# The state product k^T v of a gated linear attention, written as two 48-column matmuls in two halves of TensorE's array instead of one of 112 columns

## The chip, the cores and the metric

The kernel runs on one core of a Trainium2 chip, in one launch. The metric is the device time in microseconds, the median of several runs. A core has five engines with an instruction queue each: PE (TensorE, matrix products into PSUM), DVE (VectorE), ACT (ScalarE), POOL (GpSimd) and SP (SyncE, which here issues the DMAs). In the profile a matmul leaves two kinds of records: PEld, the load of the stationary operand into the array, and PE, the streaming of the moving operand.

## What is computed

A gated linear attention over 4 batches of 8 heads, 768 steps and 48 channels, and behind it a feed-forward layer (384 to 2048 to 384) on its 3072 tokens. Per head:

```
S_re, S_im = (ar * S_re - ai * S_im) + k[t] v[t]^T,  ar * S_im + ai * S_re
y[t] = q[t]^T S_re                    # 48 x 48 state, one step after the other
h = x @ w_in;  g = h * sigmoid(1.702 * h);  out = g @ w_out
```

## The kernel before

The complex decay is taken out of the recurrence: q and k are rotated by the running phase and scaled by the running magnitude beforehand (`prepare`). A head then has 48 cosine rows and 48 sine rows. They are put, by DMA, into rows 0 to 47 and 64 to 111 of a 112-row operand `qkh`, and rows 48 to 63 hold zeros.

The tokens are worked in 12 units of 256 (three units to a batch), each unit in two chunks of 128. For a chunk, `attend` puts these steps on PE, each in two groups of four heads (`hh`):

- scores (L690, out `p_ps`): eight matmuls a group, each 64 stationary columns, which write to partitions 0 to 63 or 64 to 127 in turn; four of them stream 128 columns and four stream 64. DVE masks the result into `pm` (L694).
- mix (L716, out `x_ps`): matmuls of 32 stationary columns, four of them in the four quarters of the array, over `pm` and the state `st`.
- turn (L736, out `k_ps`): four transposes of k, 112 rows, which ACT copies to `kt` (L745).
- zed (L742, out `z_ps`): the state product, four matmuls a group, the lines that the change touches. Each takes `kt` of a head, 112 columns wide, as the stationary operand, and streams the head's 48 columns of v, so that it writes 112 partitions by 48 columns. DVE then adds `z_ps` to the state (L750, L754). No step follows the last chunk of a batch, so there are 20 chunks with this product: 40 groups and 160 matmuls.

The feed-forward layer of a unit (`moe`) consists of L780 (`h_ps`, 128 stationary columns, 256 moving) and L810 (`o_ps`, 128 stationary, 384 moving). In unit 0 its operands are plain float32 (`x`, `valA`, `valU`, `g`); from unit 1 on both operands are split in two parts of a shorter format and three products are summed (`xhi`, `xlo`, `hiA`, `loA` and so on).

A record of PE is not a matmul: a plain float32 matmul, as in L690, L716 and L742, leaves two PE records and two PEld records, one pair for each of two passes. So a group of four in L742 has 8 records.

The order of all instructions is planned beforehand (`Plan`), by durations that stand in the code: `add("PE", 0.44, ...)` for a group of L742. The change leaves these numbers alone, and the instructions of every engine stand in the same order after it. So what stands beside a group of L742 is the same as before. Counted over the 40 groups: ahead of it comes a wide step (L736, L780 or L810, with 112 or 128 stationary columns) 31 times, L690 5 times, L716 4 times; behind it comes a wide step 23 times, L690 9 times, L716 8 times.

Of the kernel before, what the change touches and what calls it, by code (L numbers as in the profile page):

```python
# [23 lines left out]
HL = 64  # L24
T = 256
H = 8
D = 48
# [8 lines left out]
KD = 112  # L36
# [45 lines left out]
class Plan:  # L82
# [5 lines left out]
    def add(self, eng, dur, rank, fn, r=(), w=(), tab=None, name="", grp=None, work=1.0):  # L88
        n = len(self.ops)
        deps = {self.wrote[x] for x in (*r, *w) if x in self.wrote}  # L90
        for x in w:
            deps.update(self.read.pop(x, ()))
            self.wrote[x] = n
        for x in r:
            if x not in w:
                self.read.setdefault(x, []).append(n)
        deps.discard(n)
        self.ops.append((eng, dur, rank, fn, deps, tab, name, grp, work))
# [227 lines left out]
def attention_moe(ctx: ExitStack, tc: tile.TileContext, qk_in, v, a_in, w_in, w_out, qn, kn, vn, an, bn, out):  # L326
# [33 lines left out]
    kt = [sb.tile([P, 4, KD], F32, name=f"kt{i}") for i in range(1)]  # L360
# [5 lines left out]
    z_ps = ps.tile([P, H * VP], F32, name="z_ps")  # L366
# [25 lines left out]
    act, dve, pool, mm, dma = nc.scalar.activation, nc.vector, nc.gpsimd, nc.tensor.matmul, nc.sync.dma_start  # L392

    def a_t(n):
        return 0.2 + n * 0.000833
# [261 lines left out]
    def attend(u):  # L657
# [4 lines left out]
        def at(h, j, c):  # L662
            lo = j * L if len(sps) == 2 else j * T + c * L
            return qh[c if len(sps) == 2 else 0][:, h, lo : lo + L]

        def rk(o):
            return attn_rank(u, o)
# [12 lines left out]
        for c in range(2):  # L680
            vt, kv = vts[c], f"v{c}"
# [51 lines left out]
            for hh in range(2):  # L733
                def turn(c=c, hh=hh):
                    for j in range(4):
                        nc.tensor.transpose(k_ps[:, j, 0:KD], at(4 * hh + j, 1, c)[0:KD], ident[0:KD, 0:KD])  # L736

                def zed(c=c, hh=hh, vt=vt):
                    for j in range(4):
                        h = 4 * hh + j  # L740
                        lo = h * VP + h % 2 * (VP - D)
                        mm(z_ps[0:KD, lo : lo + D], lhsT=kt[0][:, j, 0:KD], rhs=vt[:, lo : lo + D], start=True, stop=True)  # L742

                add("PE", 0.35, rk(4 * c + hh), turn, r=hk[c], w=["K"], work=0.85)
                add("ACT", a_t(4 * KD) - 0.12, rk(4 * c + hh), lambda: act(  # L745
                    out=kt[0][:, :, 0:KD], in_=k_ps[:, :, 0:KD], func=AF.Copy
                ), r=["K"], w=["kt"])
                add("PE", 0.44, rk(4 * c + 2 + hh), zed, r=["kt", kv], w=["Z"], work=0.49)
# [411 lines left out]
```

## Time and profile before

| what | value |
|---|---|
| runs | 603.56 us median of 3 (603.18 to 605.73) |
| profiled execution | span 601.1 us from its first to its last instruction |
| PE busy | 567.2 us, 94% of the span |
| PEld busy | 528.5 us, 88% |
| DVE busy | 473.0 us, 79% |
| ACT busy | 272.4 us, 45% |
| granted TensorE clock | 0.996 on the mean of the span |

The span is that of one profiled execution; the three timed runs lie 2.1 to 4.6 us above it. Times of instructions are counted from the span's start. In a timeline row the first number is the start, the second the time from the first start to the last end of the records merged in the row (x8 is eight records). The ends of matmuls are modelled and overlap their successors, so what a step occupies is read from its start to the next step's start. A row of a window that begins in the middle of a group shows the group's records that are still running there, and its start is that of the first of these.

### The profile page before, as it was taken

To read this page: it belongs to the slowest core of one execution; us is meant where nothing else is said; L and a number is where in the kernel's file an instruction comes from. 1 tells how busy PE (TensorE), PEld (TensorE's weight loads), DVE (VectorE), ACT (ScalarE), POOL (GpSimd) and SP (SyncE) were. 2 spreads that over 40 slices of the span, in tenths; PEclk is the share of its full clock that TensorE was granted. 3 is DMA by queue.
4 is the path that set the end of the run, shared out by engine and by line. 5 is a ranking of instruction groups with operands and counts; after the bars stand their busy time and mean duration, and the time that the engine had idled before them with its cause. 6 is when DMAs were issued, how large, how long until landed. Compare 5 with 4: busy or idle time off the path is not lost.

```text
span 601.1 us, 13195 instructions
## 1 busy us (share of the span) xinstructions
PE 567.2 (94%) x5484; PEld 528.5 (88%) x5484; DVE 473.0 (79%) x827; ACT 272.4 (45%) x373; POOL 23.3 (4%) x75
## 2 busy tenths in 40 slices
PE   0499999999999999999999999999899999999995
PEld 0477778999989999999999999999889999999994
DVE  7999999989879778788788688788689678554433
ACT  8888477246463552732723613533542542111110
POOL 4110000000000000000000000000000000000000
PEclk9999999999999999999999999999999999999998
DMA  8488852453651740833807724742852822722211
GB/s 342 143 287 302 225 188 67 86 129 128 113 159 34 159 130 14 167 100 93 197 16 133 224 78 103 179 146 91 154 183 56 195 90 72 155 73 56 68 45 41
DMA packets 31524, 78.44 MB, mean 131 GB/s; under 512 B 4448, under 2 KB 9568, under 8 KB 31456
## 3 DMA queue, kind: packets, MB, share of 16 engines
q1 hardware_dynamic: 31456, 77.52, 47.6%
q8 instruction: 45, 0.74, 0.5%
q14 instruction: 23, 0.19, 0.1%
HBM read 53.87 MB, written 4.72 MB: 97 GB/s over the span
## 4 chain that ended last, share of the span: by engine, by line
PE 88%; DVE 3%; ACT 3%; DMA 3%; SPq 2%; issue 0%; DVEq 0%
PE h_ps L780 34%; PE o_ps L810 34%; PE x_ps L716 7%; PE p_ps L690 6%; PE z_ps L742 5%; PE k_ps L736 3%; DMA raw_w<-in_w_out_dram 1%; DMA raw<-in_w_out_dram 1%; SPq L655 1%; SPq L652 1%; DMA ri<-in_a_dram 1%; SPq L653 0%; ACT L997 0%; DVE pm L694 0%; ACT raw L462 0%; DVE s L604 0%
## 5 line engine op out<-in xcount | busy, mean ns | idle before, releaser
L780 PE MATMUL h_ps<-xhi,hiA 128*128 128x256 f32 x528 | 151.8, 287 | 0.0
L780 PE MATMUL h_ps<-xhi,loA 128*128 128x256 f32 x528 | 149.0, 282 | 0.0
L780 PE MATMUL h_ps<-xlo,hiA 128*128 128x256 f32 x528 | 149.0, 282 | 0.0
L792 ACT ACTIVATE g<-h_ps 128x512 f32<-128x512 f32 x88 | 52.6, 598 | 177.5 <-PE h_ps L780 101.0
L780 PEld LDWEIGHTS h_ps<-xhi,hiA 128*128 128x128 f32 x528 | 100.3, 190 | 1.9 <-issue 1.2
L780 PEld LDWEIGHTS h_ps<-xhi,loA 128*128 128x128 f32 x528 | 100.5, 190 | 0.0
L780 PEld LDWEIGHTS h_ps<-xlo,hiA 128*128 128x128 f32 x528 | 100.4, 190 | 0.1
L810 PE MATMUL o_ps<-hiU,gh 128*128 128x384 f32 x352 | 93.8, 347 | 0.0
L810 PE MATMUL o_ps<-loU,gh 128*128 128x384 f32 x352 | 89.7, 335 | 0.0
L810 PE MATMUL o_ps<-hiU,gl 128*128 128x384 f32 x352 | 89.6, 335 | 0.0
L810 PEld LDWEIGHTS o_ps<-loU,gh 128*128 128x128 f32 x352 | 63.7, 188 | 0.0
L810 PEld LDWEIGHTS o_ps<-hiU,gl 128*128 128x128 f32 x352 | 63.6, 188 | 0.0
L795 DVE TENSOR_TENSOR gl<-g,gh 128x512 fp32r<-128x512 f32 x88 | 60.5, 687 | 3.7
L794 DVE CAST gh<-g 128x512 fp32r<-128x512 f32 x88 | 36.9, 420 | 32.3 <-ACT g L792 21.3
L810 PEld LDWEIGHTS o_ps<-hiU,gh 128*128 128x128 f32 x352 | 57.7, 190 | 3.4 <-issue 2.6
L837 DVE TENSOR_REDUCE fit<-raw_w 128x1 f32<-128x256 f32 x96 | 37.6, 411 | 20.7 <-DMA raw_w<-in_w_in_dram 11.1
L694 DVE TENSOR_TENSOR pm<-p_ps,mask 128x512 f32<-128x512 f32 x48 | 33.0, 687 | 21.4 <-PE p_ps L690 21.3
L444 DVE TENSOR_TENSOR qk<-qk,s 128x768 f32<-128x768 f32 (+1 forms) x52 | 45.6, 890 | 3.1 <-ACT s L630 2.9
L690 PEld LDWEIGHTS p_ps<-qkh 128*64 128x64 f32 x768 | 36.7, 136 | 12.7 <-issue 5.2
L997 ACT ACT_TABLE_LOAD x36 | 46.2, 1283 | 1.4 <-PEq L1148 0.8
L690 PE MATMUL p_ps<-qkh 128*64 128x128 f32 (+1 forms) x768 | 43.5, 253 | 3.2 <-DVE pm L694 2.1
L745 ACT ACTIVATE kt<-k_ps 128x448 f32<-128x448 f32 x40 | 21.7, 543 | 42.8 <-PE k_ps L736 22.3
(94 smaller groups left out, 794.8 us busy)
## 6 DMA issues: line engine op xcount, KB each, us to landing
v<-in_v_dram SPq DMA_DIRECT2D x24, 352.0 KB, 3.9
ri<-in_a_dram SPq DMA_DIRECT2D x11, 768.0 KB, 4.9
qk<-in_qk_dram SPq DMA_DIRECT2D x11, 768.0 KB, 5.0
qkh<-qr SPq DMA_DIRECT2D x22, 288.6 KB, 5.6
qkh<-qk SPq DMA_DIRECT2D x22, 288.6 KB, 6.8
raw<-in_w_in_dram SPq DMA_DIRECT2D x8, 768.0 KB, 6.0
raw<-in_w_out_dram SPq DMA_DIRECT2D x8, 768.0 KB, 6.2
raw_w<-in_w_in_dram SPq DMA_DIRECT2D x24, 256.0 KB, 3.1
```

The source lines that it names most:

```text
L444: add(en, t, rank, lambda: e.tensor_tensor(out=out, in0=a, in1=b, op=alu), **kw)
L690: mm(p_ps[to : to + HL, j, lo:L], lhsT=at(h, 1, c)[:, lo : lo + HL], rhs=at(h, 0, c)[:, lo:L], start=True, stop=True)
L694: add("DVE", d_t(CW), rk(4 * c + hh), lambda hh=hh: dve.tensor_tensor(out=pm[hh].rearrange("p (a b) t -> p a b t", b=2), in0=p_ps.rearrang ...
L716: mm(x_ps[32 * j : 32 * j + 32, r, :], lhsT=lt, rhs=rt, start=n == 0, stop=n == len(steps) - 1)
L742: mm(z_ps[0:KD, lo : lo + D], lhsT=kt[0][:, j, 0:KD], rhs=vt[:, lo : lo + D], start=True, stop=True)
L780: mm(h_ps[hb][:, f, :], lhsT=ww[:, r * T + f * P : r * T + (f + 1) * P], rhs=x[:, r, :], start=n == 0, stop=n == last)
L792: add("ACT", a_t(CW) - 0.15, rk(i), lambda hb=hb: act(out=g32, in_=h_ps[hb], func=AF.Silu, scale=SLOPE), r=[f"h{hb}"], w=["g"], tab=SILU, ...
L794: add("DVE", d_t(CW, 2), rk(i), lambda gb=gb: dve.tensor_copy(out=high.g(gb), in_=g32), r=["g"], w=[f"gh{gb}"])
L795: add("DVE", d_t(CW), rk(i), lambda gb=gb: dve.tensor_tensor(out=glo[gb], in0=g32, in1=high.g(gb).bitcast(F32), op=ALU.subtract), r=["g", ...
L810: mm(o_ps[t], lhsT=x[:, f, t * L : (t + 1) * L], rhs=y[:, f * DM : (f + 1) * DM], start=i == 0 and f == 0 and n == 0, stop=i == NP - 1 and ...
L837: add("DVE", d_t(CK), rk + 2, lambda x=x, op=op: dve.tensor_reduce(out=f_w[:, x, n : n + 1], in_=weights.looked_at()[:, :, 1], op=op, axis ...
L997: nc.scalar.preload_act_table_set(o[5])
```

## The change

The state product of a head is written as two matmuls. `g` = 0 takes the 48 columns of `kt` that hold the cosine rows and writes partitions 0 to 47; `g` = 1 takes columns 64 to 111, the sine rows, and writes partitions 64 to 111. Both stream the same 48 columns of v. Partitions 48 to 63 of `z_ps`, which received products with zeros, are no longer written and keep the zeros that were put there at the start. A group now has 8 matmuls and 16 records.

```diff
                     for j in range(4):
                         h = 4 * hh + j
                         lo = h * VP + h % 2 * (VP - D)
-                        mm(z_ps[0:KD, lo : lo + D], lhsT=kt[0][:, j, 0:KD], rhs=vt[:, lo : lo + D], start=True, stop=True)
+                        for g in range(2):
+                            mm(z_ps[g * HL : g * HL + D, lo : lo + D], lhsT=kt[0][:, j, g * HL : g * HL + D],
+                               rhs=vt[:, lo : lo + D], start=True, stop=True)
```

Here `KD` is 112, `HL` 64, `D` 48 and `VP` 56.

## Rows read from the trace of the kernel before

**Rows 1.** The page, chain of work that ended last, share by engine.

```profile
PE 88%; DVE 3%; ACT 3%; DMA 3%; SPq 2%; issue 0%; DVEq 0%
```

**Rows 2.** By stretch: length, busy PE, PEld, DVE, ACT, POOL, clock, DMA share, GB/s.

```profile
43.00:78.00 35.00, 35.00 (x148) 25.87 (x148) 34.45 (x50) 23.66 (x31) 2.01 (x3) 1.00 0.90 270
78.00:106.00 28.00, 28.00 (x324) 23.08 (x321) 26.99 (x42) 20.76 (x29) 1.42 (x5) 1.00 0.32 114
106.00:255.00 149.00, 148.38 (x1481) 142.78 (x1481) 125.75 (x203) 73.02 (x95) 3.74 (x17) 1.00 0.47 113
```

**Rows 3.** Weight loads by shape: busy us, mean ns of one.

```profile
L690 PEld LDWEIGHTS p_ps<-qkh 128*64 128x64 f32 x768 | 36.7, 136 | 12.7 <-issue 5.2 <-DVE pm L694 2.9 <-DMA qkh<-qk 1.3
L742 PEld LDWEIGHTS z_ps<-v,kt 128*112 128x112 f32 x320 | 35.4, 177 | 1.2 <-issue 0.8
```

**Rows 4.** Timeline of PE: a group of L742 between two halves of L810.

```profile
121.75 0.51 PE L810 MATMUL o_ps<-hiU,gl 128*128 128x384 f32 x2
122.10 0.89 PE L742 MATMUL z_ps<-v,kt 128*112 128x48 f32 x8
122.81 0.60 PE L810 MATMUL o_ps<-hiU,gh 128*128 128x384 f32 x2
123.25 0.34 PE L810 MATMUL o_ps<-loU,gh 128*128 128x384 f32 x1
```

**Rows 5.** The same group, windows inside it: its second and fourth record.

```profile
122.14 0.46 PE L742 MATMUL z_ps<-v,kt 128*112 128x48 f32 x3
...
122.34 0.46 PE L742 MATMUL z_ps<-v,kt 128*112 128x48 f32 x3
```

**Rows 6.** Timeline of PE: L810 into L690, and L716 in its steady pace.

```profile
127.81 0.51 PE L810 MATMUL o_ps<-loU,gh 128*128 128x384 f32 x2
128.16 0.51 PE L810 MATMUL o_ps<-hiU,gl 128*128 128x384 f32 x2
128.61 0.89 PE L690 MATMUL p_ps<-qkh 128*64 128x128 f32 x16
129.43 0.42 PE L716 MATMUL x_ps<-pm,v 128*32 128x128 f32 x8
...
131.51 0.40 PE L716 MATMUL x_ps<-qkh,st 128*32 128x128 f32 x8
131.73 0.40 PE L716 MATMUL x_ps<-pm,v 128*32 128x128 f32 x8
```

**Rows 7.** The L690 group of 128.61, windows inside it: second, fifth, eighth pair.

```profile
128.77 0.50 PE L690 MATMUL p_ps<-qkh 128*64 128x128 f32 x6
...
129.10 0.40 PE L690 MATMUL p_ps<-qkh 128*64 128x64 f32 x8
...
129.27 0.23 PE L690 MATMUL p_ps<-qkh 128*64 128x64 f32 x2
```

**Rows 8.** Timeline of PE: L742 into L690 into L810.

```profile
207.23 0.89 PE L742 MATMUL z_ps<-v,kt 128*112 128x48 f32 x8
208.05 0.89 PE L690 MATMUL p_ps<-qkh 128*64 128x128 f32 x16
208.87 0.62 PE L810 MATMUL o_ps<-hiU,gh 128*128 128x384 f32 x2
209.32 0.51 PE L810 MATMUL o_ps<-loU,gh 128*128 128x384 f32 x2
```

**Rows 9.** Chain of waits, 75 to 107: L742 behind L690, and behind L736.

```profile
86.75 0.92 PE z_ps L742 x8
...
94.24 0.73 PE z_ps L742 x8
```

**Rows 10.** Chain of waits, 28 to 50.

```profile
34.05 5.07 DMA raw<-in_w_out_dram
...
42.24 0.40 ACT x L724
```

**Rows 11.** Chain of waits, 243 to 260.

```profile
252.53 0.64 DVE st L750
```

**Rows 12.** Chain of waits, 436 to 452.

```profile
440.12 0.69 DVE pm L694
...
442.46 0.61 DVE pm L694
```

## The prediction

> **What bounds the kernel now.** I read the chain of work that ended last first: PE holds 88% of it [rows 1], so a microsecond taken from PE is, by default, one off the time. Then the busy time by stretch, to see where another engine keeps up with PE only just: from 43 to 78 us DVE is busy 34.45 of 35.00 us, from 78 to 106 us 26.99 of 28.00, and only behind that does it have room, 125.75 of 149.00 [rows 2]. Then, for the price of the product, PE's timeline at single records, since what a group occupies is the distance between starts.
>
> **What a group of L742 costs now.** Its records follow each other at 0.10 us (122.14 to 122.34 is two records [rows 5]; over a group 0.098). That isn't the 48 moving columns; it is the weight load. Loads of 112 and 64 columns take 177 and 136 ns [rows 3], so a column costs 41 / 48 = 0.85 ns and 112 columns 96 ns. Between wide neighbours a group takes 0.71 us from its start to that of the next step (122.10 to 122.81 [rows 4]): 0.04 to the second record, six steps of 0.098, and 0.08 behind the last. Its start is not delayed: the two L810 records ahead of it take 0.35 us (121.75 to 122.10 [rows 4]), as much as two such records among themselves (127.81 to 128.16 [rows 6]).
>
> **What a group costs afterwards.** L690 is the nearest row: 64-column loads whose matmuls go in turn to the two halves. Its second half, which streams 64 columns, runs at 0.057 us for a pair of records, one in each half (129.10 to 129.27 is three pairs [rows 7]). One 64-column load is 55 ns by the 0.85, so the two halves load and stream at the same time. With 48 columns both the load and the stream shrink by a quarter, and I take 0.057 - 16 x 0.85 ns = 0.044 us a pair. The bounds are 0.057 (nothing gained below 64 columns) and 0.043 (three quarters of it). A group's first pair is longer. L690's takes 0.16 us (128.61 to 128.77 [rows 6, 7]), while its next three take 0.33 (128.77 to 129.10 [rows 7]), 0.11 each: 0.05 more, one 64-column load that nothing covers. For 48 columns that is 0.04, and the first pair takes 0.084. From first to last start that makes 0.007 + 0.084 + 6 x 0.044 = 0.355 us.
>
> **What changing the width of the tiles costs.** L810 into L690 takes 0.45 us from the start of the last two records (128.16 to 128.61) where 0.35 is the pace [rows 6]: about 0.09 while the array empties; I take the same behind L780 and L736. Out of L690 it is 0.16 behind the last pair (129.27 to 129.43 [rows 6, 7]) where the pace is 0.057: again 0.095 to 0.10. The wide step that follows also starts slower: two L810 records take 0.45 behind L690 (208.87 to 209.32 [rows 8]) and 0.44 behind L742 (122.81 to 123.25 [rows 4]); I count 0.02. Today L742 is a wide step, so it pays this toward narrow ones: into L690 a group takes 0.82 (207.23 to 208.05 [rows 8]), 0.19 behind its last record, and behind L690 it holds 0.92 of the chain where it holds 0.73 behind L736 [rows 9], which is 0.10 of waiting and 0.09 of an uncovered first load. The page "TensorEngine Tiling" of the Trainium skill (Tiling Modes, Key Properties) says that a change of the tiling mode, and not of the tile alone, drains TensorE. That speaks against this change at its wide neighbours, and the 0.09 agree with it; without them the gain summed below would be 4.5 us larger, and if L690 as a neighbour were no exception it would be 1.9 us smaller.
>
> **The sum**, over the 40 groups and their neighbours.
> - Inside: behind a wide step 0.63 becomes 0.355, -0.275 x 31 = -8.5 us. Behind L716 (another width before and after) 0.72 becomes 0.355, -0.365 x 4 = -1.5. Behind L690 the width now stays, so there is no uncovered load either: 0.72 becomes 0.007 + 7 x 0.044 = 0.315, -0.405 x 5 = -2.0. Together -12.0.
> - Ahead: +0.09 x 31 = +2.8 behind wide steps, 0 behind L716, -0.10 x 5 = -0.5 behind L690. Together +2.3.
> - Behind: toward wide steps 0.08 becomes 0.044 + 0.095 = 0.14, with the 0.02 that is +0.075 x 23 = +1.7. Toward L716 0.19 becomes 0.14, -0.05 x 8 = -0.4. Toward L690 0.19 becomes 0.05, and L690's first pair loses its 0.05: -0.19 x 9 = -1.7. Together -0.4.
>
> PE's own time falls by 10.1 us. The order of instructions is unchanged, no wait is added, and no DMA or copy changes.
>
> **What of it reaches the end.** Seven groups lie before 106 us, worth 2.0 us of the 10.1. There the gain meets other engines: the first L780 waits for an ACT copy (42.24) that stands in ACT's queue behind work on a weight DMA that landed at 39.1 [rows 10], and DVE has 0.55 us to spare up to 78 and 1.01 up to 106 [rows 2]. I count 1.7 of the 2.0 as lost. The group at 251.6 is followed by state update, decay and mask on DVE before L690 may go on (L750 at 252.53 [rows 11]), so only the part up to its last record counts: 0.2 lost. The one at 440.0 lies beside a row of DVE work that starts with the mask of the L690 group ahead of it and ends with that of the next (440.12 to 443.07 [rows 12]): all 0.4 lost. That leaves 10.1 - 2.3 = 7.8 us. The rows come from an execution with a span of 601.1 us, so 593.3 us of span; the median lies 2.5 above the span, and against it I forecast 603.56 - 7.8 = 595.8 us.
>
> **Rivals.**
> - A pair can't go below what the trace shows. L690's pairs take 0.057, and L716, with four records at a time, 0.22 us for eight (131.51 to 131.73 [rows 6]), 27 ns a record; at 0.044 a pair has 22 ns a record, which no row shows. For it: that. Against it: the 0.057 is explained by a load of 55 ns alone, and the load shrinks with its columns [rows 3]. At 0.057 with a first pair of 0.10 the inside is 0.45, so 40 x 0.094 = 3.8 us are missing and 0.4 more behind the groups: 10.1 becomes 5.9, and with 1.6 lost 4.3: 599.3 us. Chance 0.20. In the Trainium skill, "TensorE: Matmul & The Clock Gate" (Part 1, on the 56 ns) states that starts of matmuls never come closer than about 25 ns however small they are; no row here has a steady pace below 27 ns, so the trace does not contradict it.
> - A 48-column tile next to a 64-column one counts as a change of width too. For it: no row has such a pair. Against it: 48 columns don't fit in the next smaller width that the kernel uses, 32. Then L690 as a neighbour gives 5 x 0.135 + 9 x 0.14 = 1.9 us less, of which 0.4 would have been lost anyway: 6.3 instead of 7.8, 597.3 us. Chance 0.15.
> - PE runs ahead into DVE later as well. For it: 84% of DVE busy from 106 to 255 [rows 2], in an order that is fixed, so a mask or a split that was in time may come late. Against it: PE waits hardly anywhere there (148.38 of 149.00 busy). At half of the 7.8: 599.7 us. Chance 0.12.
> - Slower: the two halves take turns, because both matmuls of a head stream the same 48 columns of v and L690's do not share theirs. Place: inside each group. Then 16 records go one by one at 0.044, 0.084 + 14 x 0.044 = 0.70 instead of 0.355, and 40 x 0.345 = 13.8 us come back: 10.1 less becomes 3.7 more, 3.3 of them seen since DVE covers some of it before 106 us: 606.9 us. It decides from where a pair costs about 0.078 us (each ns on a pair adds some 0.3 us over 40 groups). For it: the shared operand. Against it: in L690 the halves plainly overlap, at 0.057 for two. Chance 0.05.
>
> **How the numbers follow.** The first account has 0.48: 595.8 us. Its own range goes from 593.4 (nothing of the 10.1 lost) to about 598. The range that should hold 8 in 10 reaches over the second, and to the floor and the DVE case: 593.4 to 600.5. About 0.5% (3 us) is what a measurement of this kernel tells from no change, so faster means below 600.5. The account, the width rival and most of the floor and DVE cases lie there, 0.87; within 0.5% I put 0.09, from the ends of these two; slower 0.04, nearly all from the halves that take turns.
>
> **What would show it.** In the profile afterwards, a group of L742 between two L810 steps has 16 records and takes about 0.50 us from its start to the next step (0.71 now), with 0.09 more ahead of it; its pairs follow at 0.044. L690 behind it starts 0.05 after its last record and has a first pair of 0.11. The shares of L742 and of L690 in the chain both fall, and the start of L780 at 42.68 hardly moves. Pairs at 0.057 or 0.088, 0.14 behind L742 toward L690, or new idle time of PE in front of L690 or L780 past 106 us would each put one of the rivals in its place. The forecast is wrong if the time lies above 600.5 or if PE's idle time grows by more than the 2.3 us counted as lost.

## The result, and the profile after

The changed kernel takes 595.91 us (median of 4 runs, 594.53 to 599.62) where the kernel before takes 603.37 us (4 runs, 602.76 to 605.73): a ratio of 0.9889, with a 95% interval of 0.9867 to 0.9911. The forecast was 595.8. The profiled execution ran 595.74 us, with a span of 594.3 us, 6.8 less than the span before.

The page of the changed kernel, share of each engine and then of each line in the chain that ended last ([rows 1] before; L743 is the state product now, L782 and L812 are the old L780 and L810):

```profile
PE 86%; DMA 4%; ACT 3%; DVE 3%; SPq 1%; issue 0%; ACTq 0%
PE o_ps L812 34%; PE h_ps L782 33%; PE x_ps L716 7%; PE p_ps L690 6%; PE z_ps L743 3%; PE k_ps L736 3%; DMA qkh<-qk 2%; DMA raw<-in_w_out_dram 1%; PE h_ps L637 1%; DMA raw_w<-in_w_in_dram 1%; DVE qk L444 1%; DMA ri<-in_a_dram 1%; DVE pm L694 1%; ACT L999 0%; ACT raw L462 0%; DVE s L604 0%
```

PE still holds most of it. What is new is `qkh<-qk`, the DMAs that bring the sine rows of q and k (rows 64 to 111) into the operand of L690.

Timeline of PE in the changed kernel, the group that stood at 122.10 [rows 4], and the one that stood at 207.23 [rows 8]:

```profile
121.12 0.51 PE L812 MATMUL o_ps<-hiU,gl 128*128 128x384 f32 x2
121.56 0.56 PE L743 MATMUL z_ps<-v,kt 128*48 128x48 f32 x16
122.06 0.62 PE L812 MATMUL o_ps<-hiU,gh 128*128 128x384 f32 x2
122.52 0.34 PE L812 MATMUL o_ps<-loU,gh 128*128 128x384 f32 x1
...
205.13 0.56 PE L743 MATMUL z_ps<-v,kt 128*48 128x48 f32 x16
205.53 0.85 PE L690 MATMUL p_ps<-qkh 128*64 128x128 f32 x16
206.31 0.62 PE L812 MATMUL o_ps<-hiU,gh 128*128 128x384 f32 x2
```

Between two L812 steps a group takes 0.50 us from its start to the next step (0.71 before), and the two L812 records ahead of it 0.44 (0.35 before): the change of width. Toward L690 it takes 0.40 (0.82 before), and L690 itself 0.78 (0.82 before).

Windows in the middle of the group at 121.56; the rows start with the group's third, ninth and eleventh record:

```profile
121.64 0.40 PE L743 MATMUL z_ps<-v,kt 128*48 128x48 f32 x10
...
121.78 0.35 PE L743 MATMUL z_ps<-v,kt 128*48 128x48 f32 x8
...
121.83 0.30 PE L743 MATMUL z_ps<-v,kt 128*48 128x48 f32 x6
```

The third record opens the second pair, at 121.64, 0.08 behind the first. From 121.78 to 121.83 is one pair, 0.045 us, in which one record of each half starts; before, one record took 0.098 [rows 5].

Weight loads of the changed kernel by shape ([rows 3] before):

```profile
L690 PEld LDWEIGHTS p_ps<-qkh 128*64 128x64 f32 x768 | 36.9, 136 | 13.7 <-issue 4.6 <-DMA qkh<-qk 3.3 <-DVE pm L694 2.8
L743 PEld LDWEIGHTS z_ps<-v,kt 128*48 128x48 f32 x640 | 17.7, 124 | 6.2 <-issue 2.9 <-ACT s L555 0.2
```

A load of 48 columns takes 124 ns by the 136 of 64: 0.75 ns a column, near the 0.85 that the shapes before gave. Twice as many loads are busy half as long together (17.7 us in place of 35.4): each is narrower (48 columns in place of 112), and two of them run at once.

Busy time by stretch, changed kernel ([rows 2] before):

```profile
43.00:78.00 35.00, 34.27 (x154) 25.11 (x155) 34.32 (x49) 23.25 (x31) 2.01 (x3) 1.00 0.93 286
78.00:106.00 28.00, 28.00 (x354) 22.71 (x349) 27.14 (x43) 21.36 (x30) 1.42 (x5) 1.00 0.33 112
106.00:255.00 149.00, 147.04 (x1595) 139.27 (x1594) 126.67 (x205) 74.50 (x97) 3.73 (x17) 1.00 0.49 116
```

PE was never idle from 43 to 78 us and now is for 0.73 us, while DVE stays full. From 106 to 255 PE's idle time grew from 0.62 to 1.96 us.

Where those waits stand, in PE's timeline of the changed kernel:

```profile
42.28 0.92 PE L782 MATMUL h_ps<-x,valA 128*128 128x256 f32 x3 [1.17 <-ACT x L724]
...
48.94 0.91 PE L812 MATMUL o_ps<-valU,g 128*128 128x384 f32 x2 [0.73 <-ACT g L790]
...
248.83 0.61 PE L690 MATMUL p_ps<-qkh 128*64 128x128 f32 x6
250.28 0.67 PE L690 MATMUL p_ps<-qkh 128*64 128x128 f32 x10 [0.84 <-DMA qkh<-qk]
250.88 0.60 PE L736 MATMUL k_ps<-ident,qkh 112*128 112x112 f32 x4
252.60 0.98 PE L690 MATMUL p_ps<-qkh 128*64 128x128 f32 x16 [1.12 <-DVE pm L694]
```

and the same place in the kernel before:

```profile
252.42 0.89 PE L690 MATMUL p_ps<-qkh 128*64 128x128 f32 x16
253.24 0.60 PE L736 MATMUL k_ps<-ident,qkh 112*128 112x112 f32 x4
254.47 0.98 PE L690 MATMUL p_ps<-qkh 128*64 128x128 f32 x16 [0.62 <-DVE pm L694]
```

PE reached this L690 3.59 us earlier than before (248.83 against 252.42). Six records on, it waits for the second of the five DMAs that fill the sine rows of `qkh`; then for the mask, in front of which DVE waited for the last of the five (L674, which scales the state by a column of `qkh`). The L690 behind that starts 1.87 us earlier than before (252.60 against 254.47). So 1.7 us of what PE had gained by then was given back at one place.

PE's earlier arrival is not all of it, since the DMAs themselves took longer. Time from issue to landing of the first two of the five (L652), in this order: the kernel before (issued at 244.34 and 244.90), the changed kernel (241.17 and 241.74), and from the experiments below `one_half` (241.31 and 241.87) and `half_by_half` (243.51 and 244.08):

```profile
DMA to landing us min/median/max: 5.3/6.1/7.0
DMA to landing us min/median/max: 7.1/7.8/8.5
DMA to landing us min/median/max: 5.3/6.1/6.8
DMA to landing us min/median/max: 7.1/7.7/8.3
```

The second was issued 3.2 us earlier than before and landed only 1.6 us earlier (250.24 against 251.86). A transfer lands in sixteen parts, and in the changed kernel one part comes 1.5 us behind the other fifteen. The kernel before has such a late part at another unit: its second DMA issued at 198 us takes 7.8 us, where the changed kernel's takes 6.7. `after_again` shows the same (8.3 us at this place, 6.4 at the other). Why the late part falls on another transfer in the changed kernel is open.

### The profile page after: what moved, and what is told of

Its sections match the earlier page's. It is cut to its first block, busy times and chain, and to the rows that moved or that the text cites. A ratio compares the mean times of both kernels' runs of the same rounds, so it can differ in the third digit from the quotient of the medians.

```text
span 594.3 us, 13835 instructions
## 1 busy us (share of the span) xinstructions
PE 557.5 (94%) x5804; PEld 512.9 (86%) x5804; DVE 472.4 (79%) x827; ACT 272.1 (46%) x373; POOL 23.8 (4%) x75
## 4 chain that ended last, share of the span: by engine, by line
PE 86%; DMA 4%; ACT 3%; DVE 3%; SPq 1%; issue 0%; ACTq 0%
PE o_ps L812 34%; PE h_ps L782 33%; PE x_ps L716 7%; PE p_ps L690 6%; PE z_ps L743 3%; PE k_ps L736 3%; DMA qkh<-qk 2%; DMA raw<-in_w_out_dram 1%; PE h_ps L637 1%; DMA raw_w<-in_w_in_dram 1%; DVE qk L444 1%; DMA ri<-in_a_dram 1%; DVE pm L694 1%; ACT L999 0%; ACT raw L462 0%; DVE s L604 0%
## 5 line engine op out<-in xcount | busy, mean ns | idle before, releaser
L782 PE MATMUL h_ps<-xhi,hiA 128*128 128x256 f32 x528 | 152.0, 288 | 0.0
L782 PE MATMUL h_ps<-xlo,hiA 128*128 128x256 f32 x528 | 149.0, 282 | 0.0
L782 PE MATMUL h_ps<-xhi,loA 128*128 128x256 f32 x528 | 149.0, 282 | 0.0
L782 PEld LDWEIGHTS h_ps<-xhi,hiA 128*128 128x128 f32 x528 | 100.2, 190 | 2.4 <-issue 1.2
L782 PEld LDWEIGHTS h_ps<-xlo,hiA 128*128 128x128 f32 x528 | 100.3, 190 | 0.3
L782 PEld LDWEIGHTS h_ps<-xhi,loA 128*128 128x128 f32 x528 | 100.5, 190 | 0.0
L812 PE MATMUL o_ps<-hiU,gh 128*128 128x384 f32 x352 | 93.9, 347 | 0.0
L812 PE MATMUL o_ps<-loU,gh 128*128 128x384 f32 x352 | 89.7, 335 | 0.0
L812 PE MATMUL o_ps<-hiU,gl 128*128 128x384 f32 x352 | 89.6, 335 | 0.0
L812 PEld LDWEIGHTS o_ps<-loU,gh 128*128 128x128 f32 x352 | 63.7, 188 | 0.0
L812 PEld LDWEIGHTS o_ps<-hiU,gl 128*128 128x128 f32 x352 | 63.6, 188 | 0.0
L812 PEld LDWEIGHTS o_ps<-hiU,gh 128*128 128x128 f32 x352 | 57.6, 190 | 3.9 <-issue 2.6
L690 PEld LDWEIGHTS p_ps<-qkh 128*64 128x64 f32 x768 | 36.9, 136 | 13.7 <-issue 4.6
L690 PE MATMUL p_ps<-qkh 128*64 128x128 f32 (+1 forms) x768 | 43.6, 253 | 4.5 <-DMA qkh<-qk 2.6
```

What stands on the lines that cost most here:

```text
L690: mm(p_ps[to : to + HL, j, lo:L], lhsT=at(h, 1, c)[:, lo : lo + HL], rhs=at(h, 0, c)[:, lo:L], start=True, stop=True)
L782: mm(h_ps[hb][:, f, :], lhsT=ww[:, r * T + f * P : r * T + (f + 1) * P], rhs=x[:, r, :], start=n == 0, stop=n == last)
L812: mm(o_ps[t], lhsT=x[:, f, t * L : (t + 1) * L], rhs=y[:, f * DM : (f + 1) * DM], start=i == 0 and f == 0 and n == 0, stop=i == NP - 1 and ...
```

## Experiments

**Only one half** (`one_half`).

```diff
-                        for g in range(2):
+                        for g in range(1):
```

> Only the cosine half (g = 0) of the state product is computed; the sine half of the state stays zero. Theory (the two halves of the array load and stream at the same time, a pair of records costs 0.045 us whatever is in the second half): a group of L743 still takes about 0.50 us between wide steps, and the time is that of the changed kernel, 596 us within 1.5. Rival (the halves take turns and each record has its own 0.022 to 0.044 us): the group shrinks by half, 0.15 to 0.30 us on each of 40 groups, and the time falls to 585 to 591.

595.40 us (ratio to before 0.9863, 0.9784 to 0.9942), against 595.91 for both halves. PE's timeline:

```profile
121.78 0.56 PE L743 MATMUL z_ps<-v,kt 128*48 128x48 f32 x8
122.27 0.62 PE L812 MATMUL o_ps<-hiU,gh 128*128 128x384 f32 x2
```

Eight records take 0.49 us where sixteen took 0.50. The second half of the array is free of charge; that the halves take turns is ruled out.

The run also shows the place at 251 us without the slow transfer (6.8 us in place of 8.5), at the same pace of PE:

```profile
248.87 0.32 PE L690 MATMUL p_ps<-qkh 128*64 128x128 f32 x1
...
251.35 0.98 PE L690 MATMUL p_ps<-qkh 128*64 128x128 f32 x16 [1.02 <-DVE pm L694]
```

PE comes 3.55 us earlier than before and does not wait for `qkh<-qk` here; the L690 behind it starts 3.12 earlier. So 0.4 us are given back in place of 1.7.

**One half after the other** (`half_by_half`).

```diff
-                    for j in range(4):
...
-                        for g in range(2):
+                    for g in range(2):
+                        for j in range(4):
```

> The same 8 matmuls of a group in another order: four in the lower half, then four in the upper. Theory (what was gained is the overlap of the two halves): with neighbours in the same half there is no overlap, 16 records follow at 0.044 us, a group takes some 0.3 us more, 40 groups some 12 us of PE, of which 1 to 3 are hidden: 605 to 608 us, slower than the kernel before. Rival (what was gained is 96 columns in place of 112 and the narrower width by itself, in any order): no difference, 596 within 1.5. Third possibility: PE reaches ahead over four matmuls and overlaps the halves all the same: 596 too, but with starts 7 ns apart between records of g = 0 and g = 1.

602.42 us (0.9974, 0.9942 to 1.0006): 6.5 us above the changed kernel, with the same matmuls. Neither the 605 nor the 596 that I had expected. PE's timeline:

```profile
121.92 0.78 PE L743 MATMUL z_ps<-v,kt 128*48 128x48 f32 x16
122.63 0.62 PE L812 MATMUL o_ps<-hiU,gh 128*128 128x384 f32 x2
```

A group takes 0.71 us, 0.21 more than the changed kernel's and less than the 0.3 of no overlap; over 40 groups 8.4 us of PE, of which 6.5 arrived. Record by record the lower half runs alone for two matmuls, then both halves run together, then the upper half runs alone. So PE does reach ahead to the other half, but not over four matmuls. Nearly the whole gain hangs on the order g inside j. At 251 us PE comes only 1.0 us earlier than before, yet with the slow transfer (8.3 us) it gives back 1.3.

**Every group twice** (`twice`).

```diff
-                    for j in range(4):
+                    for j in (0, 1, 2, 3, 0, 1, 2, 3):
```

> Every group of the state product is issued twice (the second pass writes the same values over the first), 16 more records of 0.022 us at the same width: 0.36 us a group and 14.4 us of PE in all, with no other engine touched. Theory (PE is the bound nearly everywhere behind the first 100 us, and so four fifths or more of what PE gains or loses there reaches the end): 595.9 plus 10.5 to 13.5, 606 to 609.5 us. Rival (DVE and the DMAs into qkh set the pace as much as PE, and the 10 us that PE lost were seen only in part for that reason): half or less arrives, 603 us or below.

607.46 us (1.0051, 1.0022 to 1.0079), 11.6 above the changed kernel of 14.4 us added: 0.80 arrives, and what is missing is again at the places named above: before 106 us and at 250 and 430 us PE's added work went into waits that the changed kernel has anyway. PE's timeline at 254:

```profile
253.92 0.92 PE L743 MATMUL z_ps<-v,kt 128*48 128x48 f32 x32
254.67 0.85 PE L690 MATMUL p_ps<-qkh 128*64 128x128 f32 x16
255.46 0.60 PE L736 MATMUL k_ps<-ident,qkh 112*128 112x112 f32 x4
257.04 0.98 PE L690 MATMUL p_ps<-qkh 128*64 128x128 f32 x16 [0.98 <-DVE pm L694]
```

There is no wait for `qkh<-qk` here now: PE comes late enough.

**The changed kernel again** (`after_again`).

> The changed kernel once more, beside the next three. Theory (the stalls in front of L690 at 250 and 428 us come from the order: PE runs up to the DMAs that fill qkh in two of the twelve units): PE waits there again, 1 to 2.5 us each, and the median is 595 to 597 us. Rival (they were an accident of one execution): no wait over 0.3 us at one or both of these places.

595.38 us (0.9849, 0.9792 to 0.9907). PE's longest waits behind its start (who waited for what: us in total, times, longest):

```profile
PE p_ps L690 <- DMA qkh<-qk: 2.2, 3, 1.3
PE p_ps L690 <- DVE pm L694: 1.8, 4, 1.0
PE h_ps L782 <- ACT x L724: 1.4, 1, 1.4
```

The waits at 250 and 429 us are there again (0.63 and 1.32 us for the DMA). They belong to the kernel, not to one execution. The 0.73 us at 48.94 is missing this time, though the 1.39 at 42 is longer.

**The inspection of the weights cut down, before and after** (`light_before`, `light_after`). Both leave out most of a test of the weights' range; the order of instructions stays.

```diff
-            out=weights.looked_at().bitcast(I32).rearrange("p n w -> p (n w)"),
-            in_=src[j // per].bitcast(I32)[:, j % per * 2 * CK : (j % per + 1) * 2 * CK],
+            out=weights.looked_at().bitcast(I32).rearrange("p n w -> p (n w)")[:, 0:16],
+            in_=src[j // per].bitcast(I32)[:, j % per * 2 * CK : j % per * 2 * CK + 16],
...
-                out=f_w[:, x, n : n + 1], in_=weights.looked_at()[:, :, 1], op=op, axis=AX.X, apply_absolute_value=True
+                out=f_w[:, x, n : n + 1], in_=weights.looked_at()[:, 0:8, 1], op=op, axis=AX.X, apply_absolute_value=True
```

> The kernel before with the inspection of the weights cut down: each of its 96 DVE reductions looks at 8 words a partition in place of 256, and each of the 48 DMAs brings 16 words in place of 512. The order stays; some 30 us of DVE work and 12 MB of DMA go. This run and light_after form a pair. Theory (PE sets the time nearly alone): it loses only its waits in front of L690 at 254 and 433, 600 to 603 us.

> The changed kernel with the inspection cut down in the same way. Theory (of PE's 10.2 us, 1.4 are lost before 106 us to DVE's conversion of weights, which stays, and the other 2 us lost are lost to DVE and DMA behind it): against light_before it gains 8.3 to 9.2 us, more than the 7.5 of the full kernels, 592 to 594 us, with the waits at 250 and 428 gone or under 0.5 us. Rival (the loss has nothing to do with DVE's load or the extra DMAs): the difference of the pair is 6.5 to 7.7 us and the waits stay.

602.07 us (0.9964, 0.993 to 0.9999) and 593.12 us (0.9822, 0.9762 to 0.9882): the pair differs by 8.95 us, where the full kernels differ by 7.5. DVE's busy time is 448.7 and 448.1 us in place of 473.0 and 472.4. PE's timeline of `light_after` at the two places:

```profile
248.79 0.57 PE L743 MATMUL z_ps<-v,kt 128*48 128x48 f32 x16
249.18 1.30 PE L690 MATMUL p_ps<-qkh 128*64 128x128 f32 x16
250.41 0.60 PE L736 MATMUL k_ps<-ident,qkh 112*128 112x112 f32 x4
251.93 0.98 PE L690 MATMUL p_ps<-qkh 128*64 128x128 f32 x16 [0.91 <-DVE pm L694]
...
426.69 0.89 PE L690 MATMUL p_ps<-qkh 128*64 128x128 f32 x16
427.51 0.60 PE L736 MATMUL k_ps<-ident,qkh 112*128 112x112 f32 x4
428.38 0.98 PE L690 MATMUL p_ps<-qkh 128*64 128x128 f32 x16 [0.26 <-DVE pm L694]
```

The wait for the DMA is gone at 427, and at 249 it is down to 0.45 us (the group takes 1.23 in place of 0.78); the second DMA takes 7.7 us there in place of 8.5, and 0.7 us are given back in place of 1.7. So by the medians 1.5 us of the change's loss go with the inspection's DVE work and DMAs (1.2 if `after_again` and the kernel before beside it, 603.16 us, are taken for the full kernels), from single runs that spread over 2.5 to 3.2 us. Which of the two matters more was not tried, since both were cut together. The wait for the mask at 251.93 stayed at 0.91, against what I had expected.

**A planner that knows the widths** (`plan_by_width`).

```diff
+                pick = min(can[e], key=lambda x: x[0] + (TURN if ops[x[1]][7] != width else 0.0))
...
+            if e == "PE" and ops[n][7] != width:
+                dur += DRAIN
...
+TURN = 1.0
+DRAIN = 0.1
```

> The changed kernel with a planner that knows the width of PE's steps (64 for L690 and the state product, 32 for L716, 128 for the rest): it adds 0.1 us where the width changes and takes a step of the same width first if one is ready within 1 us of rank; the state product has 0.36 us in place of 0.44. Changes of width on PE fall from 205 to 177. Theory (each change of width costs about 0.1 to 0.14 us of PE): 28 x 0.12 = 3.4 us less of PE, 592 to 595 us. Rival (the order was tuned with the old numbers against stalls of DVE and DMA that no planner number shows, and a new order finds new ones): 596 to 603.

600.03 us (0.9933, 0.9895 to 0.9971), 4 us slower than the changed kernel by the medians, although PE is busy 554.9 us in place of 557.5. The theory's 592 to 595 us fails, and the time lies in the rival's range. PE's longest waits behind its start, in the same columns:

```profile
PE p_ps L704 <- DVE pm L708: 3.1, 4, 1.7
PE x_ps L730 <- DVE pm L708: 3.1, 5, 1.5
PE o_ps L826 <- DVE osb L837: 0.8, 1, 0.8
PE p_ps L704 <- DMA qkh<-qk: 0.7, 1, 0.7
PE k_ps L750 <- ACT kt L761: 0.6, 1, 0.6
```

A whole new order moves the masks and the copies of `kt` too, and PE meets them late. The profiled run is the fastest of the ten (597.42 us, mean granted clock 0.998); others had a lower one, down to 0.987 (601.57 us). So the waits show why 2.6 us of PE brought nothing, and the rest of the 4 us stands in no trace.

**Only the state product moved** (`beside_scores`, `beside_scores_late`), with the changed kernel beside the second (`after_beside_late`). A group is taken out of PE's finished order and put where fewer changes of width are left; all else keeps its place.

```diff
+        for z in [n for n in order if ops[n][6] == "Z"]:
...
+                    if z in ops[n][4] or n in ops[z][4]:
+                        break
...
+                    if t < best and (found is None or (t, seen) < found[:2]) and cost(new) <= base + 0.02:
+                        found = t, seen, new
```

> The changed kernel with its order kept except for groups of the state product: each is moved past at most five PE steps where that saves changes of width (205 become 186) and the planner's own time does not rise. Theory (a change of width costs 0.10 to 0.14 us of PE, and most of it reaches the end when nothing else is moved): 19 x 0.12 = 2.3 us less of PE, 593 to 595 us. Rival (as in plan_by_width: moved steps meet kt, the state or a mask too late): 596 or above, with new waits of PE in front of L743 or behind it.

595.58 us (0.9848, 0.9789 to 0.9908), no better than the 595.38 of `after_again` beside it. PE's busy time is 1.5 us less (556.0 against 557.5). What spoiled the profiled run stands at 43 us. Windows of `beside_scores`, with the granted clock behind the five engines:

```profile
42.00:42.90 0.90, 0.00 (x0) 0.00 (x0) 0.90 (x3) 0.90 (x3) 0.23 (x1) 0.97 0.93 366
42.90:46.00 3.10, 3.00 (x7) 2.47 (x8) 3.10 (x5) 2.26 (x5) 1.78 (x3) 0.50 1.06 412
46.00:49.00 3.00, 3.00 (x14) 2.59 (x14) 2.96 (x7) 2.97 (x4) 0.00 (x0) 0.96 1.01 413
```

PE waited 2.5 us for ACT's copy there, and behind that wait the granted clock is 0.50, the lower of its two levels (1.2 of 2.4 GHz), for 3.1 us: 7 records where `after_again` has 16.

> As beside_scores, but the groups of unit 0 stay where they were (188 changes of width in place of 205). In beside_scores PE waited 2.5 us in front of the first L780 (1.4 in after_again), the granted clock fell to 0.50 behind that wait, and L780 was 2.4 us behind after_again at 43.8; from there to 340 us the moved groups won 2.4 us back. Theory (the moves win 17 x 0.12 = 2.0 us of PE, and only the start of the feed-forward layer spoiled it): no clock below 0.9 at 43 us, and 593 to 594.5 us, 1 to 2 us below the changed kernel in the same job. Rival (what is won ahead of a stall at 250 or 428 is waited there again): within 0.6 us of the changed kernel.

> The changed kernel, to compare beside_scores_late with on the same chip: 595 to 596 us. PE waits in front of L690 at 250 and 428 us again, 1 us or more with what follows.

With unit 0 left alone: 594.52 us (5 runs, 593.32 to 596.03; 0.9829, 0.9803 to 0.9855) against 596.84 (5 runs, 595.50 to 597.72; 0.9872, 0.9849 to 0.9896) for the changed kernel. That is 2.3 us by the medians (2.0 worked out), with intervals that just overlap. The one execution that was profiled is its slowest (596.03 us), and its span of 594.3 shows nothing of it (594.1 for the other). The clock at 43 us is 1.00. It leads by 1.4 us at 340 and still by 0.9 at 429, behind two waits for `qkh<-qk` (0.56 and 1.02 us, where the other waits once, 1.54). But then the clock falls:

```profile
429.30:432.60 3.30, 3.30 (x44) 2.74 (x44) 2.24 (x5) 0.54 (x1) 0.03 (x1) 0.50 0.59 169
```

At 433.4 the lead is gone, so most of it went at the lower clock and not in the waits. The runs' mean granted clocks fit: 593.32 to 594.52 us at 0.995 to 0.997 and 595.88 and 596.03 at 0.993, against 595.50 and 595.96 (0.996 and 0.997) and 596.84 to 597.72 (0.993 and 0.994) for the changed kernel. So I take it as the fastest version here, likely but not firmly shown.

## Why the prediction was right, point by point

**What a group costs.** The pace of a pair was worked out as 0.044 us and is 0.045; the first pair 0.084 and 0.080; the change of width 0.09 ahead of wide neighbours and 0.095 behind, measured 0.44 - 0.35 and, from the last record at 121.92 to 122.06, 0.14 in place of 0.08. Between L812 steps the account gives -0.110 us a group, the traces -0.105; from L736 to L716 -0.235 and -0.238; from L690 to L736 -0.43 and -0.43. The floor at 0.057 a pair is refuted: 22.5 ns a record is held steadily. Whether the load (48 columns, 41 ns by the 0.85) or the stream sets these 45 ns a pair was not tried. With 22.5 ns a record, the page "TensorE: Matmul & The Clock Gate" of the Trainium skill (Part 1, on the 56 ns), by which starts never come closer than about 25 ns, doesn't hold for records in two halves.

**Neighbours of width 64.** L690 and the 48-column product count as the same width, as assumed: 0.04 us behind the last record toward L690, where a change takes 0.14. One small part was over-estimated. L690's first pair behind L743 lost 0.035 us of its 0.16 where I counted 0.05; over 9 groups 0.1 us.

**The sum for PE.** The 40 differences, each taken from the last record ahead of a group to the fourth or fifth behind it, add up to 9.8 us over the 39 that hold no wait in the kernel, and to 10.1 with the two at 47.97 and 94.08 (one waits itself, one is followed by a wait for `xlo`) put at their neighbours' 0.11. Forecast: 10.1.

**What reaches the end** was right as a sum (2.3 us lost; 2.6 by the medians, 3.4 in the pair of profiled executions) and partly wrong as to place. Part of the agreement is luck: the forecast put the median 2.5 us above the profiled span, which was 2.3 before (603.37 - 601.1) and is 1.6 now (595.91 - 594.3). Before 106 us 1.4 were lost (1.7 forecast): L782 waits 1.17 in place of 0.61 for the same ACT copy, and part of what is left is waited at 48.94. At 440 us the chain of DVE work decides as described; the wait in front of L716 there is 0.4 us more. At 430 us the same wait was there before, and PE's lead is the same ahead of it and behind it (4.6 us), so nothing new was lost.

At 251 us I had counted 0.2 us, for the state update ahead of the mask, and 1.7 were lost. Two steps failed here. One read this place off the chain before: [rows 11] shows the DVE work, and it was the last to arrive then, but only just. L674 on DVE starts behind both the state update and the DMAs into `qkh`; before, the update ended at 253.15 and DVE had the last of the DMAs (landed at 252.80) at 253.07, 0.1 us of margin. `one_half`, with transfers as fast as before, gives back 0.4 us. The other step is that "no DMA or copy changes": the second DMA took 8.5 us in place of 7.0, and 1.3 of the 1.7 us go with that (1.0 of 1.5 in `after_again`). PE's need for it alone left room before, since it landed at 251.86 and the record that reads it started at 252.80. I had looked for waits that are there, not for those that stand next to zero, and had not asked what the changed kernel does to the transfers.

The prediction's second sign of being wrong was PE's idle time growing by more than the 2.3 us. It grew by 2.9 us in the profiled pair (33.9 to 36.8), and in the two other profiled runs of the changed kernel by 1.9 and 2.7. So the account of what is lost failed by its own sign in two executions of three, although the time came out. L690's share of the chain did not fall either; it is 6% before and after.

**The rivals.** Halves that take turns: refuted by `one_half`. A floor for the pair and a change of width toward L690: refuted by the records. PE running into DVE later: a small part of it is true, 0.4 us at one place by `one_half`. The slower transfer is a loss that no rival named.

## What to carry to other kernels

A matmul with few moving columns (48 here, against 112 stationary ones) costs its weight load, so two narrow loads in two halves of the array are cheaper than one wide one, if matmuls of different halves stand next to each other in the order; put the loop over the halves innermost. Each change of width at the edges of such a group cost about 0.1 us and an uncovered first load, so a narrow group belongs beside others of its width, and it is worth moving that group alone rather than planning everything anew. When PE is to become faster, look not only for its waits but for operands that land just as it arrives, and read in the trace afterwards whether the transfers still take as long: here a late part moved from one transfer to another and cost 1.3 us.

## What the runs showed of the hardware that I had not expected

- Two loads of the stationary operand run at once in two column halves, and so steadily that 16 records with 8 products in each half take no longer than 8 in one (0.50 and 0.49 us).
- PE overlaps the halves over a distance of a few records only: in `half_by_half` the upper half started two matmuls late and ended two late.
- In `beside_scores` a wait of 2.5 us in front of a matmul stream was followed by 3.1 us at a granted clock of 0.50; waits of 1.2 to 1.4 us at the same place were not. In `beside_scores_late` two waits of 0.56 and 1.02 us with six records between them were followed by 3.3 us at 0.50, while a single wait of 1.75 us at that place in the changed kernel was not.
- One transfer into `qkh` took 8.5 us in the changed kernel and 7.0 before, because one of its sixteen parts landed 1.5 us behind the rest; `after_again` (8.3) and `half_by_half` (8.3) have it too, `one_half` (6.8) does not.
